# Routed attention followed by a channel mix: moving the weight loads, two cluster products and the token shift within the loop

## Chip, cores and metric

One core of a Trainium2 chip. The metric is the device time of one execution in microseconds (us). Ratios are the mean time of one kernel's fast runs over that of the other's fast runs of the same rounds, so not quite the ratio of the medians quoted. A run counts as slow when it lies over 1.5% above the fastest of its kernel.

## The reference, cut to what matters

```python
# attention over 4 batches x 8 heads, 768 positions, head_dim 64, 16 clusters a head
q_assign = argmax(normed(q) @ normed(centroids).T); k_assign = the same of k
mask   = q_assign[:, None] == k_assign[None, :]
x      = softmax(where(mask, q @ k.T / 8, -1e9)) @ v      # -> (4, 768, 512)
# channel mix
x_prev = x shifted by one position
xk, xr = mu_k * x + (1 - mu_k) * x_prev,  mu_r * x + (1 - mu_r) * x_prev
k      = maximum(xk @ w_k, 0)
out    = sigmoid(xr @ w_r) * (k * k @ w_v)
```

The mask is made by arithmetic: each position's cluster, as 16 one-hot rows, is appended to q and k ("aug"), so the score matmul adds a bonus where clusters agree.

## The kernel before

Heads go in 16 pairs. The loop has 192 steps of one score product (two matmuls, lines 286 and 287), one exponential and six value matmuls; a pair n takes steps 12n to 12n+11. Everything else is hung on step numbers: `at(t, f)` puts f at the end of step t, `forced[t]` in its middle. That makes the order of the code for each engine and each issuing queue. Slices of the channel mix fill PE from step 58 on.

```python
at(6, load_mu)                                   # two 2 KB vectors, SP's queue
for i in range(4):
    at(9 + i, load_wk, i)                        # key weights: cast to bf16, issued by GpSimd
    at((19, 20, 28, 29)[i], load_wv, 2 * i)      # value weights
for i in range(2):
    at(37 + i, load_wr, 2 * i)                   # receptance weights
...
for n in range(NPAIR):
    s = n * W                                    # W = 12
    ...
    # a: steps (from s) of four DVE transposes of pair n+2's q and k, and of its cluster products
    if n == NP:       a = (8, 9, 10, 11, 14)     # NP = 4
    elif n == NP + 1: a = (3, 4, 5, 6, 10)
    elif n == NP + 2: a = (1, 2, 3, 4, 8)
    else:             a = (-1, 0, 1, 2, 5)
    for g in range(4): at(s + a[g], trans, n + 2, g)
    forced[s + a[4]] = lambda n=n: aff_mm(n + 2) # on PE, reads all four transposes
    d = a[4] - 4
    at(s + 5 + d, aff_max, n + 2)                # DVE: maximum, comparison
    at(s + 6 + d, aff_back, n + 2, [nc.sync])    # DVE transpose, then four one-hot transfers on SP
    at(s + 8, load_v, n + 2, nc.sync)
    ...
    e = s + W + NCH                              # = s + 18
    at(e, xt_dma, n); x = e + 4                  # pairs 4 to 14 (the change leaves 7 and 11 at e + 4)
    at(x, sh); at(x + 1, sh2)                    # token shift on DVE: six instructions
```

(Cut: the first pairs' own paths, where PE transposes.)

The softmax here doesn't subtract the row's maximum and nothing guards it: scores larger than these inputs give would overflow.

## Time and profile before

| | before |
|---|---|
| time, median of 4 runs | 255.16 us (253.51 to 257.03) |
| span of the profiled run | 254.8 us |
| PE, ACT, DVE busy | 95%, 74%, 69% |
| mean granted TensorE clock | 0.993 |

The shares are averages over stages with different limits; what counts is which wait ends last in a stage. I therefore read the profile in stretches of twelve steps, bounded by the starts of the score matmuls of line 286. The prediction shows these stretches.

### The profile page before, as it was taken

What the parts mean: (1) busy time and instruction counts of PE and PEld (TensorE: products, weight loads), DVE (VectorE), ACT (ScalarE), POOL (GpSimd) and SP (SyncE); (2) the same over time, 40 slices, a digit from 0 to 9 for tenths busy, and PEclk for the clock granted to TensorE, in tenths of its full rate; (3) what the DMA queues carried; (4) which work ended last, traced back from release to release, by engine and by line L of the source; (5) the groups of instructions that cost most, each with busy time, mean ns of one, the idle gap of its engine ahead of it and who ended that gap; (6) DMA issues with size and microseconds to landing.
All of it is one profiled execution on the core that took longest, in us unless ns stands there. A gap on an engine that the chain in (4) does not pass through costs nothing.

```text
span 254.8 us, 6199 instructions
## 1 busy us (share of the span) xinstructions
PE 243.2 (95%) x2356; PEld 148.2 (58%) x2387; DVE 176.6 (69%) x375; ACT 189.7 (74%) x271; POOL 94.0 (37%) x186
## 2 busy tenths in 40 slices
PE   7999979999999999999999999999999999999994
PEld 3866747766665554555666655555666555555441
DVE  3476765998999979676979877767776356554222
ACT  4298967989998867787889986878999887146210
POOL 2877867581644263543261607070701000000000
PEclk9999997999999999999999999999999999999999
DMA  6782999798938385869674949496222112120122
GB/s 177 210 238 32 199 279 244 126 140 147 185 46 162 57 159 102 162 158 195 157 115 108 129 104 204 119 193 104 74 47 65 44 71 73 47 79 0 56 110 85
DMA packets 102318, 31.88 MB, mean 125 GB/s; under 512 B 74704, under 2 KB 98704, under 8 KB 102288
## 3 DMA queue, kind: packets, MB, share of 16 engines
q1 hardware_dynamic: 98352, 28.03, 52.6%
q0 software_dynamic: 2208, 2.62, 6.4%
q10 hardware_dynamic: 1728, 0.82, 1.2%
q8 instruction: 19, 0.31, 0.5%
q14 instruction: 11, 0.09, 0.1%
HBM read 24.15 MB, written 6.29 MB: 119 GB/s over the span
## 4 chain that ended last, share of the span: by engine, by line
PE 74%; DMA 8%; ACT 7%; DVE 4%; issue 3%; POOL 2%; SPq 1%; DVEq 0%; ACTq 0%
PE psv L405 16%; PE st L286 13%; PE out L299 11%; PE psr L394 8%; PE psk L382 8%; PE st L287 6%; ACT pt L289 6%; DMA qk_nat<-in_q_dram 4%; PE affps L194 4%; PE psk L373 4%; DMA qk_rows<-in_q_dram 2%; PE trps L161 2%; DVE qkT L145 1%; DMA cn_sb<-in_centroids_dram 1%; POOL aug L175 1%
## 5 line engine op out<-in xcount | busy, mean ns | idle before, releaser
L289 ACT ACTIVATE pt<-st 128x768 bf16<-128x768 f32 x192 | 148.4, 811 | 26.0 <-PE st L287 25.5
L175 POOL TENSOR_SCALAR aug<-qkT 64x384 bf16<-64x384 f32 x128 | 68.3, 533 | 85.5 <-DVE qkT L145 58.5
L299 PEld LDWEIGHTS <-pt 128*128 128x128 bf16 x1152 | 60.4, 97 | 27.2 <-ACT pt L289 1.7
L286 PE MATMUL st<-aug 80*128 80x512 bf16 x192 | 73.7, 384 | 1.6 <-ACT pt L289 0.5
L299 PE MATMUL out<-vt,pt 128*128 128x65 bf16 x1152 | 66.6, 193 | 1.1 <-ACT pt L289 0.8
L287 PE MATMUL st<-aug 80*128 80x256 bf16 x192 | 52.2, 272 | 0.0
L405 PE MATMUL psv<-w_v_sb,k 128*128 128x512 bf16 x181 | 46.3, 378 | 0.8 <-ACT tanh L397 0.2
L387 ACT ACTIVATE kr<-psk 128x512 bf16<-128x512 f32 x48 | 28.8, 600 | 8.6 <-PE psk L382 4.7
L409 DVE SCALAR_TENSOR_TENSOR out_sb<-tanh,psv 128x512 f32<-128x512 bf16 x24 | 16.3, 680 | 27.1 <-PE psv L405 26.6
L382 PE MATMUL psk<-xk,w_k_sb 128*128 128x512 bf16 x113 | 30.6, 378 | 0.7
L388 DVE TENSOR_TENSOR k<-kr 128x512 bf16<-128x512 bf16 x48 | 21.9, 459 | 13.4 <-ACT kr L387 13.3
L286 PEld LDWEIGHTS <-aug 80*128 80x128 bf16 x192 | 18.8, 98 | 16.3 <-issue 8.4
L397 ACT ACTIVATE tanh<-psr 128x512 bf16<-128x512 f32 x24 | 14.3, 597 | 18.1 <-PE psr L394 14.6
L405 PEld LDWEIGHTS <-k 128*128 128x128 bf16 x192 | 16.8, 97 | 16.8 <-issue 2.0
L287 PEld LDWEIGHTS <-aug 80*128 80x128 bf16 x192 | 19.1, 99 | 9.9 <-issue 1.7
L394 PE MATMUL psr<-w_r_sb,xr 128*128 128x512 bf16 x91 | 23.7, 379 | 0.2
L182 POOL CAST vt<-v_nat 128x384 bf16<-128x384 f32 x32 | 16.3, 539 | 14.2 <-DMA v_nat<-in_v_dram 13.3
L145 DVE STREAM_TRANSPOSE qkT<-qk_nat 128x384 f32<-128x384 f32 x40 | 20.6, 550 | 0.0
L312 DVE TENSOR_TENSOR xn<-out,rs 128x384 bf16<-128x384 f32 x32 | 17.8, 557 | 1.1
L373 PE MATMUL psk<-xk,w_k_sb 128*128 128x256 bf16 x128 | 16.6, 272 | 0.4 <-DVE out_sb L409 0.4
L382 PEld LDWEIGHTS <-w_k_sb 128*128 128x128 bf16 x128 | 11.2, 97 | 9.3
L194 PE MATMUL affps<-qkT,cblk 128*32 128x384 f32 (+1 forms) x144 | 15.6, 445 | 0.0
(64 smaller groups left out, 196.4 us busy)
## 6 DMA issues: line engine op xcount, KB each, us to landing
v_nat<-in_v_dram SPq DMA_DIRECT2D x16, 384.0 KB, 4.0
out_dram<-out_sb SPq DMA_DIRECT2D x24, 256.0 KB, 2.6
qk_nat<-in_q_dram SPq DMA_DIRECT2D x40, 96.0 KB, 4.0
qk_nat<-in_k_dram SPq DMA_DIRECT2D x40, 96.0 KB, 3.5
qk_rows<-in_q_dram SPq DMA_DIRECT2D x5, 384.0 KB, 5.6
qk_rows<-in_k_dram SPq DMA_DIRECT2D x4, 384.0 KB, 6.2
aug<-oht SPq DMA_DIRECT2D x60, 24.0 KB, 1.9
w_k_sb<-in_moe_w_k_dram POOLq DMA_DIRECT2D x4, 256.0 KB, 5.8
```

Source lines behind the costliest of these rows:

```text
L145: nc.vector.transpose(qkT[n][:, g, :], nat[n][:, g // 2, (g % 2) * GW:(g % 2 + 1) * GW])
L175: nc.gpsimd.tensor_scalar(augv(n, g)[0:64, par, :], in0=qkT[n][64 * par:64 * par + 64, g, :], scalar1=qk_scale, scalar2=1.0, op0=ALU.mult, ...
L194: nc.tensor.matmul(ps[32 * g:32 * g + 32, u], cblk[:, 2 * j + g % 2, :, :], qkT[n][:, g, u], start=True, stop=True, tile_position=(0, 32 * g))
L286: nc.tensor.matmul(st[:, 0:512], kc, a[rows, 0:512], start=True, stop=True)
L287: nc.tensor.matmul(st[:, 512:S], kc, a[rows, 512:S], start=True, stop=True)
L289: nc.scalar.activation(pt, st, AF.Exp, bias=-BIG, scale=BIG)
L299: nc.tensor.matmul(o[:, (qc + NCH // 2) % NCH, :], pts[bh * NCH + c][:, qc * 128:(qc + 1) * 128], vts[n % NR][:, tt, 2 * (c % 3) + c // 3, ...
L373: nc.tensor.matmul(ps[:, a * 256:(a + 1) * 256], w_k_sb[:, j, (i + a) * 128:(i + a + 1) * 128], self.xk[:, j, 512:768], start=(j == 0), st ...
L382: nc.tensor.matmul(ps, w_k_sb[:, j, ii * 128:(ii + 1) * 128], self.xk[:, j, 0:512], start=(j == 0), stop=(j == NJ - 1))
L387: nc.scalar.activation(kr, src, AF.Relu)
L394: nc.tensor.matmul(ps, self.xr[:, j, sl], w_r_sb[:, j, :], start=(j == 0), stop=(j == NJ - 1))
L405: nc.tensor.matmul(self.psvt, self.k2[:, i, sl], w_v_sb[:, i, :], start=(i == 0), stop=(i == NI - 1))
```

## The change

Its intent: load the key weights while the DMA engines are nearly idle (52 GB/s in 19 to 26 us of the profile before, 191 in 26 to 32), so that pair 4's rows come in time; give pair 8's and 9's transposes time before PE needs them; move DVE work (the token shift) away from them.

```diff
-    krp = ctx.enter_context(tc.tile_pool(name="krp", bufs=3))
+    krp = ctx.enter_context(tc.tile_pool(name="krp", bufs=5))
...
-            at(9 + i, load_wk, i)
-            at((19, 20, 28, 29)[i], load_wv, 2 * i)
+            at(7 + i // 2, load_wk, i)
+            at((27, 28, 39, 40)[i], load_wv, 2 * i)
...
-            at(37 + i, load_wr, 2 * i)
+            at(50 + i, load_wr, 2 * i)
...
-                        a = (1, 2, 3, 4, 8)
+                        a = (1, 2, 3, 4, 9)
+                    elif n == NP + 3:
+                        a = (0, 1, 2, 3, 8)
...
-                x = e + 4
+                x = e + (4 if n % NP == NP - 1 else 7)
```

## The prediction

> **What bounds the kernel now.** I counted the loop's steps by the score matmuls of line 286: one starts each step, 192 in all, then a tail without them. Their start times in the timeline give the borders of every twelve steps, and the view of engine busy time by windows gives what filled each stretch. Columns: length of the stretch, busy time of PE, weight loads, DVE, ACT and POOL, granted TensorE clock, DMA share, GB/s. Here are steps 12, 24, 36, 48, 60, 72, 84, 96 and 108 with the twelve steps that follow each:
>
> ```profile
> 22.46:32.51 10.05, 10.05 (x138) 6.89 (x139) 7.00 (x15) 8.97 (x13) 9.04 (x17) 1.00 0.84 152
> 32.51:45.60 13.09, 11.18 (x135) 7.98 (x131) 8.97 (x16) 8.95 (x13) 9.55 (x18) 0.87 1.14 260
> 45.60:55.43 9.83, 9.56 (x135) 6.85 (x131) 9.15 (x18) 9.18 (x13) 6.71 (x12) 1.00 0.76 124
> 55.43:64.34 8.91, 8.15 (x103) 5.55 (x102) 8.03 (x20) 8.83 (x13) 2.12 (x4) 1.00 0.95 149
> 64.34:78.77 14.43, 14.27 (x146) 8.64 (x148) 14.26 (x32) 12.88 (x19) 9.07 (x17) 1.00 0.67 109
> 78.77:94.37 15.60, 15.29 (x142) 9.01 (x144) 13.15 (x29) 12.54 (x19) 6.49 (x12) 1.00 0.67 119
> 94.37:108.31 13.94, 13.66 (x132) 7.74 (x132) 11.50 (x24) 9.89 (x14) 5.34 (x10) 1.00 0.71 145
> 108.31:122.22 13.91, 13.80 (x140) 7.84 (x139) 10.20 (x23) 11.26 (x16) 5.00 (x10) 1.00 0.78 164
> 122.22:135.29 13.07, 12.91 (x138) 8.24 (x140) 10.98 (x25) 11.69 (x18) 5.47 (x10) 1.00 0.70 133
> ```
>
> The reader is to see three regimes. Up to step 60 a step takes about 0.76 us, and ACT's exponential (811 ns by the page, a little less when two run together) sets it. From step 60 a step with a slice of the second operator takes 1.37 us and one without takes 0.51; PE is busy throughout, and this goes on to the end. Between them lie the odd stretches: 32.51 to 45.60 costs 3 us more than either neighbour, and 78.77 to 94.37 costs more than the same work later. PE being "busy" there hides waits inside a group of matmuls.
>
> Next, the waits in 30 to 46 us, the timeline at step 26, and the windows cut around it:
>
> ```profile
> PE trps L161 <- DMA qk_rows<-in_q_dram: 1.6, 1, 1.6
> ...
> 36.27 0.41 PE L161 MATMUL trps<-ident,qk_rows 128*128 128x128 f32 x2 [1.64 <-DMA qk_rows<-in_q_dram]
> ...
> 34.30:37.83 3.53, 1.89 (x29) 1.51 (x27) 2.21 (x4) 1.78 (x3) 1.97 (x3) 1.00 1.18 272
> 37.83:41.24 3.41, 3.41 (x28) 2.59 (x24) 1.70 (x4) 2.29 (x4) 2.26 (x4) 0.50 1.15 271
> 41.24:45.60 4.36, 4.35 (x66) 2.85 (x63) 3.44 (x7) 3.35 (x6) 3.70 (x7) 1.00 1.12 220
> ```
>
> PE stands still for 1.64 us until pair 4's query rows land, and the next 3.41 us run at half the clock. One late transfer is paid for twice.
>
> Why it is late shows in the DMA view of 26 to 32 us, and in the timeline where PE meets pair 8:
>
> ```profile
> q0 software_dynamic: 506, 0.94, 93.4%
> q1 hardware_dynamic: 350, 0.19, 11.0%
> ...
> 88.26 2.05 PE L194 MATMUL affps<-qkT,cblk 128*32 128x384 f32 x8
> 88.68 0.14 PEld L194 LDWEIGHTS affps<-qkT,cblk 128*32 128x32 f32 x2 [0.28 <-DVE qkT L145]
> 89.48 0.14 PEld L194 LDWEIGHTS affps<-qkT,cblk 128*32 128x32 f32 x2 [0.66 <-DVE qkT L145]
> ```
>
> Just before and while the rows are issued (30.52), the software queue, which carries the key weights, holds 93% of the DMA engines' time; the rows move only from about 32.5. In 19 to 26 us the same view shows 52 GB/s: the engines were almost idle there. The last two lines are the second place: the cluster products of pair 8 wait for DVE's transposes.
>
> [...] their issues cost POOL time: 562 ns median for the key weights here.
>
> **The change, part by part.** *Key weights at steps 7 and 8 rather than 9 to 12.* Same four issues, another place. In POOL's program order two now come before the value casts of pair 1 and two just after. From the timeline POOL ends the casts ahead of them at 21.5, so the issues fall at about 21.6 to 22.9 and 23.9 to 25.1, against 23.8 to 25.0 and 27.9 to 29.0. The software queue moved 0.94 MB in 6 us; 1 MB needs about 6 us, plus 1.5 us for the 384 KB of values in between. Landed by about 31 (estimate) instead of 34.7. *The value weights* leave steps 19, 20, 28, 29 for 27, 28, 39, 40, so none is in the way before step 27; *the receptance weights* go to step 50. *Pair 4's rows behind pair 2's one-hot transfers:* in the program order of SP they stand there already, with and without the change; this part costs and gains nothing. Issued at 30 to 30.5, the rows should need what a less loaded transfer needed: 3.5 us (issued 9.8, landed 13.3) to 4.1 us (14.6 to 18.6). That is 33.8 to 34.5; PE comes for them at 36.27 - 1.64 = 34.6. So the stall goes, or shrinks to a few tenths, and with it the half clock. The worth: 13.09 minus the neighbours' mean (10.05 + 9.83) / 2 = 9.94 makes 3.15; I take 2.8 for the thin margin. POOL's own delay of 1.3 us at step 7 falls on casts needed at steps 18 and 24: beside other work.
>
> *Cluster products of pair 8 one step later (81 for 80).* Steps 72 to 84 hold eight slices and one set of products, like steps 96 to 108: 15.60 - 13.91 = 1.7 us of excess. By step starts, 1.3 of it is at step 80 and 0.3 at step 78, where ACT waits for DVE to free a buffer (0.7 us, ACT kr L387 <- DVE k L388). One step is worth 1.37 us if it carries a slice and DVE has the same work ahead of the last transpose, so nearly all of the wait is covered. *The kr ring of 5* takes away that ACT wait. I count 1.4 for the two.
>
> *Pair 9: transposes one step later, products three steps later (92 for 89).* Steps 84 to 96: seven slices and products, like steps 108 to 120 at 13.07; 13.94 - 13.07 = 0.87. I count 0.7. *The token shift three steps later* adds no work. It moves about 3 us of DVE work behind the one-hot chain and spares DVE's wait for the transposed tile (2.1 us in 78 to 95), so it helps the same two places and is not counted again.
>
> Sum: 2.8 + 1.4 + 0.7 = 4.9 us. All of it lies on the path, since every step after follows PE or ACT in order, and the steps from 96 on are unchanged.
>
> **The rivals.** *First: the rows stay late.* The key weights start only 2.2 us earlier, and the one-hots and values share the engines with them. If the weights still flow at 31, the rows land near 35.5, one microsecond of stall remains and perhaps the half clock: gain 2.5 to 3 in all, time about 253. For it: a margin of at most 0.8 us. Against: the idle engines before 26 us, and no value weights at 31.35. *Second: the displaced weights hurt what they now meet.* The later value and receptance weights now share 45 to 58 us with pair 6's rows in small pieces, which feed DVE, the busiest engine there (14.26 of 14.43). If DVE's transposes come 1 to 2 us late, time is about 252.5. Against: pair 6 landed before 60 and DVE took it up at 63.84, behind its own queue. *Third: DVE is the bound from 46 to 92 us*, so the later products only meet the same transposes: steps 72 to 84 would gain 0.4 rather than 1.4, time about 252. *Fourth: all of it works fully* (3.15 + 1.7 + 0.87, and a little at step 70): about 250.
>
> **Range and chances.** The profiled execution took 256.6 us by its own time, so 4.9 less is 251.7. The three timed runs average 255.4, and part of their spread (253.51 to 257.03) may be whether the half clock struck, worth up to 1.7; taking half of 1.2 as already absent leaves 255.4 - 4.3 = 251.1. I say 251.2, nearer the second, as timed runs are what counts. Two per cent under 255.74 is 250.6, half a microsecond below my value, so faster by over 2% is somewhat less likely than not. Slower needs a new stall of 10 us with the gains, which nothing suggests. Range 248.8 to 253.9.
>
> **What would show it right or wrong.** Right: no PE wait for qk_rows between 30 and 40 us, no half-clock window there, steps 24 to 36 in about 10 us, the eight products of pairs 8 and 9 back to back in 0.85 to 1.0 us, steps 72 to 84 in about 14.2 and 84 to 96 in about 13.2, and everything from step 96 as long as before. Wrong: software-queue traffic still at 31 us with PE waiting on the rows; a new wait at step 36, 48 or 60 on a one-hot or on pair 6; or DVE idle time replaced by DVE lateness at step 81. If timed runs before never saw the half clock, my gain is too large by 0.6.

## The result, and the profile after

264.18 us median of 4 runs (262.35 to 264.83), ratio 1.034 (95% interval 1.025 to 1.043): slower. The profiled run's span is 263.1 us, 8.2 more than before.

The windows view of the kernel after, by its own steps 12, 24, 48, 60, 72, 84, 96 and 120 (columns as in the prediction):

```profile
21.84:34.45 12.61, 10.28 (x139) 6.98 (x140) 9.25 (x20) 9.16 (x12) 8.12 (x17) 1.00 0.96 179
34.45:45.72 11.27, 10.99 (x131) 7.89 (x132) 6.85 (x12) 8.54 (x12) 8.58 (x16) 0.85 0.93 207
...
55.55:67.34 11.79, 8.15 (x102) 5.50 (x102) 10.15 (x24) 9.48 (x13) 3.68 (x8) 0.99 1.14 173
67.34:82.81 15.47, 15.15 (x145) 8.99 (x149) 12.14 (x26) 12.34 (x18) 9.39 (x18) 0.90 0.70 110
82.81:96.75 13.94, 13.78 (x143) 8.63 (x144) 12.93 (x28) 12.43 (x19) 6.67 (x12) 1.00 0.72 134
96.75:110.04 13.29, 13.10 (x131) 7.51 (x132) 10.36 (x21) 9.77 (x14) 5.45 (x10) 1.00 0.80 165
110.04:126.00 15.96, 14.63 (x140) 7.98 (x139) 12.89 (x26) 11.26 (x16) 5.15 (x10) 1.00 0.60 132
...
139.07:155.36 16.29, 14.87 (x144) 8.88 (x144) 11.37 (x24) 12.97 (x20) 5.39 (x10) 1.00 0.62 93
```

Lengths against before, stretch by stretch: steps 12 to 24 +2.56, 24 to 36 -1.82, 48 to 60 +2.88, 60 to 72 +1.04, 72 to 84 -1.66, 84 to 96 -0.65, 96 to 108 +2.05, 120 to 132 +2.36, 132 to 144 +1.28, 144 to 156 +0.35; start, first steps and tail together -0.2; the rest is equal. The sum is the 8.2 of the spans. Two things are to be seen: gains came where they were forecast (72 to 96, and in part 24 to 36), and losses came in three other places: at step 24, at step 60, and at step 101 with three later steps like it.

**Two waits for one-hots.** The timeline of the kernel after, at the first score matmuls of steps 24 and 60 (in brackets the idle time before, and what ended it):

```profile
34.45 0.38 PE L286 MATMUL st<-aug 80*128 80x512 bf16 x1 [2.01 <-DMA aug<-oht]
...
67.34 0.61 PE L286 MATMUL st<-aug 80*128 80x512 bf16 x1 [2.92 <-DMA aug<-oht]
```

Its chain of waits around both (start, length, what):

```profile
26.86 0.51 SPq L219
27.43 6.93 DMA aug<-oht
...
60.31 6.98 DMA aug<-oht
```

The two transfers of 24 KB took 6.93 and 6.98 us. Pair 4's rows, which were late before, are in time now; pair 2's one-hots, issued just ahead of them on SP's queue, have become the late ones, and so have pair 5's. With each wait came a half-clock window again: the granted clock was 0.50 from 36.30 to 39.71 us and from 67.02 to 70.43 (0.85 over steps 24 to 36, 0.90 over 60 to 72). The DMA view tells what stood before pair 2's one-hots. Before, in 22.2 to 29.5 us (count, KB each, median us from issue to landing):

```profile
v_nat<-in_v_dram SPq DMA_DIRECT2D x1, 384.0 KB, 3.6
aug<-oht SPq DMA_DIRECT2D x5, 24.0 KB, 3.8
mu_k_sb<-in_moe_mu_k_dram SPq DMA_DIRECT2D x1, 2.0 KB, 2.3
mu_r_sb<-in_moe_mu_r_dram SPq DMA_DIRECT2D x1, 2.0 KB, 2.3
```

After, in 21.5 to 29.2 us:

```profile
v_nat<-in_v_dram SPq DMA_DIRECT2D x1, 384.0 KB, 10.9
aug<-oht SPq DMA_DIRECT2D x5, 24.0 KB, 6.6
mu_k_sb<-in_moe_mu_k_dram SPq DMA_DIRECT2D x1, 2.0 KB, 5.7
mu_r_sb<-in_moe_mu_r_dram SPq DMA_DIRECT2D x1, 2.0 KB, 5.9
```

mu went out before the key weights in the kernel before, and its four-byte packets were through in 2.3 us. Now the key weights flow at that moment: their issues start at 21.0 us and mu's at 21.7, where before mu's started at 22.4 and theirs at 23.8.

**DVE before pair 10's products.** The timeline before, around step 101:

```profile
107.75 0.36 DVE L349 TENSOR_TENSOR diff<-xt 128x384 bf16<-128x384 bf16 x1 [0.36 <-DMA xt<-xn]
...
110.96 1.49 DVE L145 STREAM_TRANSPOSE qkT<-qk_nat 128x384 f32<-128x384 f32 x3
...
114.05 0.85 PE L194 MATMUL affps<-qkT,cblk 128*32 128x384 f32 x8
```

And after:

```profile
111.77 1.03 DVE L145 STREAM_TRANSPOSE qkT<-qk_nat 128x384 f32<-128x384 f32 x2
112.72 0.49 DVE L349 TENSOR_TENSOR diff<-xt 128x384 bf16<-128x384 bf16 x1
...
115.07 0.56 DVE L145 STREAM_TRANSPOSE qkT<-qk_nat 128x384 f32<-128x384 f32 x1
...
117.23 0.56 DVE L145 STREAM_TRANSPOSE qkT<-qk_nat 128x384 f32<-128x384 f32 x1
117.85 0.14 PEld L194 LDWEIGHTS affps<-qkT,cblk 128*32 128x32 f32 x2 [1.92 <-DVE qkT L145]
```

The token shift of pair 6 stood ahead of all four transposes of pair 10; now it stands between the second and the fourth, and PE waits for the fourth. The same order costs 2.4 us at step 125, 1.3 at 137 and 0.35 at 149.

### The profile page after: what moved, and what is told of

Read it like the earlier page. It is cut to its first block, busy times and chain, and to the rows that moved or that the text cites. A ratio compares the mean times of both kernels' runs of the same rounds, so it can differ in the third digit from the quotient of the medians.

```text
span 263.1 us, 6208 instructions
## 1 busy us (share of the span) xinstructions
PE 244.4 (93%) x2356; PEld 148.4 (56%) x2387; DVE 181.1 (69%) x375; ACT 189.7 (72%) x271; POOL 94.4 (36%) x186
## 4 chain that ended last, share of the span: by engine, by line
PE 67%; DVE 13%; DMA 11%; issue 4%; SPq 2%; ACT 1%; DVEq 0%; ACTq 0%
PE psv L405 13%; PE st L286 11%; PE psk L382 9%; PE out L299 8%; DMA aug<-oht 6%; PE psr L394 5%; PE st L287 5%; PE psk L373 5%; PE affps L194 4%; DMA qk_nat<-in_q_dram 3%; DVE qkT L145 2%; SPq L219 2%; PE wps L446 2%; DVE out_sb L409 2%; DVE oht L217 1%
## 5 line engine op out<-in xcount | busy, mean ns | idle before, releaser
L409 DVE SCALAR_TENSOR_TENSOR out_sb<-tanh,psv 128x512 f32<-128x512 bf16 x24 | 16.3, 679 | 28.5 <-PE psv L405 27.2
L388 DVE TENSOR_TENSOR k<-kr 128x512 bf16<-128x512 bf16 x48 | 21.2, 444 | 18.5 <-ACT kr L387 18.4
L382 PE MATMUL psk<-xk,w_k_sb 128*128 128x512 bf16 x113 | 31.2, 385 | 0.9 <-issue 0.2
L286 PEld LDWEIGHTS <-aug 80*128 80x128 bf16 x192 | 18.9, 98 | 21.7 <-issue 11.3
L397 ACT ACTIVATE tanh<-psr 128x512 bf16<-128x512 f32 x24 | 14.4, 599 | 18.3 <-PE psr L394 17.4
L405 PEld LDWEIGHTS <-k 128*128 128x128 bf16 x192 | 16.8, 97 | 17.2 <-issue 2.4
L182 POOL CAST vt<-v_nat 128x384 bf16<-128x384 f32 x32 | 16.3, 539 | 20.7 <-DMA v_nat<-in_v_dram 19.9
L145 DVE STREAM_TRANSPOSE qkT<-qk_nat 128x384 f32<-128x384 f32 x40 | 21.4, 556 | 0.0
L194 PE MATMUL affps<-qkT,cblk 128*32 128x384 f32 (+1 forms) x144 | 16.5, 445 | 3.0 <-DVE qkT L145 3.0
```

The lines of the kernel that those rows point to most:

```text
L145: nc.vector.transpose(qkT[n][:, g, :], nat[n][:, g // 2, (g % 2) * GW:(g % 2 + 1) * GW])
L194: nc.tensor.matmul(ps[32 * g:32 * g + 32, u], cblk[:, 2 * j + g % 2, :, :], qkT[n][:, g, u], start=True, stop=True, tile_position=(0, 32 * g))
L286: nc.tensor.matmul(st[:, 0:512], kc, a[rows, 0:512], start=True, stop=True)
L382: nc.tensor.matmul(ps, w_k_sb[:, j, ii * 128:(ii + 1) * 128], self.xk[:, j, 0:512], start=(j == 0), stop=(j == NJ - 1))
L405: nc.tensor.matmul(self.psvt, self.k2[:, i, sl], w_v_sb[:, i, :], start=(i == 0), stop=(i == NI - 1))
```

## The experiments

Lengths in us of the stretches that differ, from each run's own profile (one profiled execution each), and the timed ratio:

| run | 0-12 | 12-24 | 24-36 | 48-60 | 60-72 | 72-84 | 84-96 | 96-108 | 120-156 | ratio (95% interval) |
|---|---|---|---|---|---|---|---|---|---|---|
| before | 10.4 | 10.1 | 13.1 | 8.9 | 14.4 | 15.6 | 13.9 | 13.9 | 40.9 | 1 |
| after | 10.7 | 12.6 | 11.3 | 11.8 | 15.5 | 13.9 | 13.3 | 16.0 | 44.9 | 1.034 (1.025-1.043) |
| e1_weights_only | 10.4 | 11.9 | 9.7 | 11.2 | 16.8 | 15.2 | 14.4 | 13.9 | 40.9 | 1.005 (0.998-1.013) |
| e2_shift_only | 10.4 | 10.1 | 13.2 | 8.9 | 14.9 | 15.1 | 14.4 | 15.1 | 44.9 | 1.013 (1.004-1.021) |
| e3_products_ring | 10.4 | 10.1 | 12.9 | 9.1 | 14.7 | 14.4 | 13.8 | 18.5 | 40.9 | 1.007 (0.998-1.016) |
| e4_products_ring_shift45 | 10.4 | 11.5 | 14.8 | 8.9 | 14.7 | 13.9 | 13.3 | 14.9 | 41.2 | 0.993 (0.981-1.004) |
| h1_weights_free_queue | 12.0 | 10.1 | 10.0 | 11.3 | 14.7 | 15.5 | 14.3 | 13.9 | 41.4 | 1.014 (0.999-1.029) |
| h2_weights_wr_back | 10.4 | 12.5 | 9.7 | 9.9 | 15.6 | 15.2 | 14.1 | 13.9 | 40.9 | 1.008 (0.999-1.016) |
| h3_pair8_ring_shift4 | 10.4 | 11.1 | 15.2 | 9.3 | 14.5 | 13.9 | 14.8 | 13.9 | 40.9 | 1.006 (0.994-1.019) |
| h4_pair8_wk_first | 14.5 | 12.0 | 9.7 | 8.9 | 14.7 | 13.9 | 14.8 | 13.9 | 40.9 | 1.013 (1.004-1.021) |
| k1_weights_v_on_act | 10.7 | 16.8 | 11.5 | 12.0 | 16.3 | 15.1 | 14.0 | 13.9 | 40.9 | 1.031 (1.023-1.040) |
| k2_wk_mu_v_on_act | 10.5 | 10.1 | 10.3 | 9.0 | 14.9 | 15.5 | 14.0 | 13.9 | 40.9 | 0.994 (0.986-1.001) |
| k3_repaired | 10.3 | 10.1 | 10.1 | 8.9 | 14.9 | 13.9 | 13.3 | 14.9 | 40.9 | 0.990 (0.985-0.996) |
| k4_repaired_pair10 | 10.3 | 10.1 | 9.9 | 9.3 | 14.8 | 13.9 | 13.3 | 13.9 | 40.9 | 0.977 (0.970-0.984) |

A warning on the ratios: the kernel before itself ran between 253.1 and 261.1 us in the later rounds. Its runs at a granted clock of 0.997 or more took 253.1 to 255.9, those at 0.986 or 0.987 took 257.5 to 260.2, and the wait at steps 24 to 27 is as changeable: e4 and h3, which load the weights as before, took 26.3 and 26.2 us for steps 12 to 36 where the profile of before had 23.1 (for e4 that puts the profiled run, 258.97 us, among its slow ones; only its later stretches are used). Differences under 1% are therefore read from the stretches, not from the ratio. All runs were correct.

### One part at a time

**e1_weights_only**: the kernel before with the three weight lines of the diff.

> The kernel before with the weight moves alone (key weights at steps 7 and 8, value weights at 27, 28, 39, 40, receptance weights at 50). Theory Q (queue order: weights on the software queue starve the small packets on SP's queue, and pair 2's and pair 5's one-hot transfers wait behind them): a wait of about 2.5 us at step 24 and about 3.5 us at step 60, each followed by a half-clock window, the stall at step 26 gone; about 5 us slower than before. Rival D (the whole loss comes from the token shift on DVE): the same time as before or 2 to 3 us faster, as the prediction had it.

Measured: waits at steps 21 and 23 (1.1 and 0.8 us over the length before), 59 and 60; the wait at step 26 gone; half clock only after step 60 (the run's granted clock was 0.987). The weights alone take 3.0 us more than before from the first to the last step. Of the first two, step 21 is DVE waiting 0.7 us for mu, with PE behind it, and step 23 the one-hots (0.7 us). So a loss comes from the weights, of 3 rather than 5 us. Rival D falls by these waits in the trace; the timed ratio alone, 1.005 (0.998 to 1.013), would not exclude it.

**e2_shift_only**: `x = e + (4 if n % NP == NP - 1 else 7)` and nothing else.

> The kernel before with the token shift three steps later and nothing else. Theory S (the shift now lies on DVE between the transposes of the pair two later and the products that need them): waits of PE for DVE at steps 101, 125, 137 and 149 that sum to about 6 us, and some more at step 89, where the products of pair 9 have not been moved here; 6 to 8 us slower. Rival Q alone (all loss from the weights): the same time as before, or up to 1 us faster.

Measured: steps 96 to 108 +1.2, 120 to 156 +4.0, in sum 5.2 us, at exactly the steps named, and 0.4 more in 84 to 96. Timed, 1.3% slower, about 3 us: less than the 6 to 8 expected. In the traces the shift is the largest single loss.

**e3_products_ring**: pair 8's and 9's tuples and the ring of 5.

> The kernel before with the products of pairs 8 and 9 later and the ring of five, shift and weights untouched. If the prediction's steps for these parts are right, steps 72 to 84 shrink by about 1.5 us and 84 to 96 by about 0.7 us: 2 us faster than before. If DVE is the bound there and the products only meet the same transposes, under 0.7 us faster.

Steps 72 to 84 shrink by 1.2; 84 to 96 hardly; and, not expected by either theory, steps 96 to 108 grow by 4.6. A half-clock window (113.9 to 117.3 us; the run's granted clock was 0.987) is part of that. Its waits in 100 to 125 us:

```profile
DVE diff L349 <- DMA xt<-xn: 2.6, 1, 2.6
```

The later products of pair 9 put their DVE chain (maximum, comparison, transpose: about 2.1 us by the durations in the timelines) and a wait for pair 6's transposed tile in front of pair 10's transposes. So the products of pair 9 moved on their own cost more at step 101 than they bring at 89.

**e4_products_ring_shift45**: the same with

```diff
-                x = e + 4
+                x = e + (7 if n in (NP, NP + 1) else 4)
```

> As the run with products and ring, with the shift three steps later for pairs 4 and 5 alone, whose products' deadlines were moved too. Theory S: no waits at steps 101, 125, 137, 149, and up to 0.5 us faster than without the shift. If a later shift hurts wherever it stands: slower than without it by 1 us or more.

Steps 120 to 144 are as before; 144 to 156 lose 0.3 (DVE waited 0.6 us for the transfer that frees an output buffer, as in h1, without any late shift); 72 to 96 as short as in the kernel after; 96 to 108 at 14.9. Steps 96 to 108 are about 3.6 us shorter than in e3, far more than the 0.5 us expected, so most of e3's loss needed the shift of pairs 4 and 5 at its old place as well as pair 9's later products. A later shift is good for pairs 4 and 5 and bad for the later ones, as theory S says; against its expectation, a wait of 1 us is left at step 101.

### What held the one-hots

**h1_weights_free_queue**: e1 with `at(4, load_mu)` and pair 2's `load_v` on `nc.scalar` at step 8.

> The weight moves alone, with the two mu vectors loaded at step 4 (while the engines are idle) and pair 2's values loaded through ACT's queue, so that nothing large stands before pair 2's one-hot transfers on SP's queue; the key weights flow at the same time as in the weights-only run. Theory Q (the one-hots were late because they stood behind mu and values on the same queue): the one-hots land 4 to 5 us after issue, as in the kernel before, no wait at steps 21 and 24; steps 12 to 24 take 10.0 to 10.6 us instead of 11.9; the wait at step 60 stays. Rival R (the engines are simply full with weights, whatever the queue): the one-hots land as late as before, near 33 us, and steps 12 to 24 still take 11.5 us or more.

Steps 12 to 36 take 20.0 us, no half clock (granted clock 1.000); theory Q's part held. But steps 0 to 12 grew by 1.7: ACT issued the values at 18.2 us, before pair 1's one-hots, for which PE then waited 1.9 us at step 12. The transfer that was taken off the queue met other one-hots instead. The wait at 59 stayed, as expected.

**h2_weights_wr_back**: e1 with `at(37 + i, load_wr, 2 * i)`.

> The weight moves with the receptance weights back at steps 37 and 38. If the receptance weights at step 50 make pair 5's one-hots late: the waits at steps 59 and 60 fall from 3.5 us in sum to under 1 us and there is no half-clock window after 60 us. If the value weights at 39 and 40 do: they stay. The wait at step 24 stays in both.

Steps 48 to 60 fell from 11.2 to 9.9 and 60 to 72 from 16.8 to 15.6, but not to 8.9 and 14.4, and a half-clock window stayed (the run's granted clock was 0.993): between the two answers expected. Of e1's 4.6 us of loss in 48 to 72, 2.4 went. So the receptance weights at 50 make about half of it. The rest is put down to the value weights at 39 and 40: no run moves these alone, but h4 and k2, with both moved back, keep at most 0.5 us of it.

**h4_pair8_wk_first**: h3 (below) with `at(3 + i // 2, load_wk, i)`, `at(4, load_mu)` and value weights at 27 to 30.

> As the run before it, and the key weights at steps 3 and 4, with mu before them and the value weights at 27 to 30: the weights then flow in the idle stretch before pair 2's values and one-hots are issued. If the prediction's idea was right and only its place on the queue wrong: no wait for pair 4's rows at step 26, no half clock there, at most 0.5 us more at step 12 because pair 1's one-hots meet the weights; 2.5 to 3.5 us faster than the run before it. If not: pair 1's one-hots land 2 us or more late and step 12 pays what step 26 gains.

The bad case came: pair 1's one-hots had nothing large before them on their own queue (mu stood there, but had landed by about 20 us, when the one-hots began to go out), and still took 5.8 us (its DMA view in 17.5 to 21.5 us), where 1.9 was usual:

```profile
aug<-oht SPq DMA_DIRECT2D x4, 24.0 KB, 5.8
```

Steps 0 to 12 grew by 4.1 us. Rival R is thus partly right: beside the running stream of weights these small transfers took 5.8 us even on a free queue. The rest of the idea held: no wait at 24 or 26 (12 to 24 took 12.0 us, which I put down to a half clock after the wait at step 12; the run's granted clock was 0.984).

**k1_weights_v_on_act**: e1 with only pair 2's values moved, to ACT at step 12.

> The weight moves alone, with pair 2's values taken off SP's queue: issued by ACT at step 12, after pair 1's one-hots are through (in the run with the free queue they were issued at 18.2 us and met those one-hots instead). mu stays where it was. Queue order (Q): pair 2's one-hots land within 4 us of issue, steps 0 to 12 take 10.4 us, steps 12 to 24 at most 10.6, 24 to 36 under 10, with no half clock there; the wait at step 60 stays. If the place of the values was not what held the one-hots: step 24 still waits over 1.5 us.

My expectation failed, in an informative way: steps 12 to 24 took 16.8 us. mu, still on SP's queue at step 6, now shared the engines with two streams: in 21 to 29 us the software queue with the key weights held 61.5% of the engines' time, ACT's queue with the values 17.3%, SP's 10.3%. Its DMA view in 21 to 29 us, and its waits in 24 to 40 us:

```profile
mu_k_sb<-in_moe_mu_k_dram SPq DMA_DIRECT2D x1, 2.0 KB, 6.1
mu_r_sb<-in_moe_mu_r_dram SPq DMA_DIRECT2D x1, 2.0 KB, 10.3
```

```profile
DVE mu_r_sb L508 <- DMA mu_r_sb<-in_moe_mu_r_dram: 4.7, 1, 4.7
PE xtps L327 <- DVE qkT L169: 4.7, 1, 4.7
```

A vector of 2 KB took 10.3 us, DVE stood before it for 4.7 us, and PE behind DVE. The four-byte packets of mu were at the head of the queue, and the values, one-hots and rows behind them; taking away the values alone did not help.

### Settling and repairing

**h3_pair8_ring_shift4**: the kernel before with pair 8's tuple, the ring of 5, and the shift later for pair 4 alone.

> The kernel before with pair 8's products one step later, the ring of five, and the shift three steps later for pair 4 alone; pair 9 and all later pairs untouched. Theory: moving pair 9's products put their DVE chain in front of pair 10's transposes, and that was the loss at step 101; so here steps 96 to 108 take 13.9 us as before and steps 72 to 84 take 13.9 to 14.4: 1 to 1.7 us faster than before in the trace. Rival: pair 10's wait comes from elsewhere and steps 96 to 108 stay above 14.8.

Steps 96 to 108 are back at 13.9 and 72 to 84 at 13.9: the wait at step 101 did come from pair 9's products. But 84 to 96 grew to 14.8, since pair 9's products, left at step 89, now wait for transposes behind pair 8's later chain. The waits hand on from pair to pair; the trace is no faster than before, as it also fell on a bad wait at step 26.

**k2_wk_mu_v_on_act**: key weights at 7 and 8, mu on ACT's queue at step 6, pair 2's values on ACT's queue at step 12, value weights at 27 to 30, receptance weights at 37 and 38.

> A repair of the weight moves: key weights at 7 and 8, mu and pair 2's values on ACT's queue, value weights at 27 to 30, receptance weights at 37 and 38 as before. If both waits are told rightly (step 24: SP's queue held; step 60: weights issued after 50 us): no wait at 24, 26, 59 and 60, no half clock, steps 12 to 36 together 19.7 to 20.6 us instead of 23.1, steps 48 to 60 8.9 us; about 2.5 to 3 us faster than the kernel before. If weights in flight hurt whatever their queue: one of these waits stays, and the time is that of before.

Steps 12 to 36 take 20.3 us against 23.1, 48 to 60 are as before, and every run was at a clock of 0.999 or more (252.75 to 254.03 us). Both waits are gone. This confirms that order and company on the queues made them, not the earlier key weights as such. It is a repair in several parts at once: mu went out on ACT's queue at 16.8 us and was through in 2.4 us, before the first key weights at 20.6, so its new time may count as much as its new queue. Timed, k2 is 0.6% faster, inside the noise (0.986 to 1.001), not the 2.5 to 3 us expected.

**k3_repaired**: k2's weights with e4's products, ring and shift.

> The same repair of the weights together with pair 8's and pair 9's products later, the ring of five and the shift later for pairs 4 and 5 alone. If the parts add: steps 12 to 36 about 20 us, steps 72 to 108 about 42.1 us, nothing lost after step 108; 3.5 to 4.5 us faster than the kernel before, the fastest of all. If they don't: at best the better of the two parts alone.

252.47 us median (251.92 to 253.23), ratio 0.990. The parts add in the trace (72 to 108: 42.1 us); timed, the gain is 1%, about 2.5 us, less than the 3.5 to 4.5 us expected.

**k4_repaired_pair10**: k3 with

```diff
+                    elif n == NP + 4:
+                        a = (-1, 0, 1, 2, 6)
```

> The repaired version with pair 10's products one step later too (step 102 for 101). Theory: the wait of 1 us left at step 101 is pair 10's last transposes, which stand on DVE behind pair 9's one-hot chain since pair 9's products come three steps later; one step of 1.37 us covers it: steps 96 to 108 take 13.9 us instead of 14.87, nothing new later, about 0.9 us faster than the repaired version. Rival: DVE is the bound there and the wait moves to step 102 or to pair 11 at step 113: the same time.

251.22 us median of 6 runs (250.46 to 252.59) beside 259.33 for all 11 runs of before in the same rounds (255.85 to 260.13); ratio of the fast runs 0.977. Windows of k3 for steps 96 to 108:

```profile
102.64:117.51 14.87, 14.74 (x142) 7.97 (x139) 11.95 (x26) 11.26 (x16) 5.37 (x10) 1.00 0.62 131
```

And of k4 for steps 12 to 36 and 72 to 108:

```profile
21.04:31.10 10.06, 10.06 (x139) 6.90 (x139) 7.38 (x15) 9.10 (x13) 9.08 (x18) 1.00 0.85 171
31.10:41.04 9.94, 9.54 (x135) 6.82 (x132) 8.37 (x16) 8.66 (x13) 7.06 (x13) 1.00 1.11 251
...
74.93:88.87 13.94, 13.94 (x146) 8.64 (x144) 13.03 (x28) 12.44 (x19) 7.21 (x12) 1.00 0.72 133
88.87:102.16 13.29, 13.21 (x133) 7.51 (x132) 10.37 (x21) 9.77 (x14) 5.46 (x10) 1.00 0.82 175
102.16:116.07 13.91, 13.91 (x142) 7.72 (x139) 11.17 (x25) 11.26 (x16) 5.03 (x10) 1.00 0.68 140
```

This version beats the kernel before clear of noise (0.970 to 0.984), and with it the kernel after. The wait of a microsecond at step 101 is gone and did not move on.

## Why the prediction was wrong, step by step

The sum was 4.9 us gained, with nothing lost elsewhere. Three of its steps failed: that the token shift "adds no work" and leaves "the steps from 96 on" unchanged (6.0 us lost), that the displaced weights cost nothing (3.9 us lost in 48 to 72), and that the order on SP's queue "costs and gains nothing" (2.6 us lost in 12 to 24). Together that is 12.5 us, more than the "new stall of 10 us" that nothing seemed to suggest.

**The wait at step 26.** "So the stall goes" was right: pair 4's rows landed in time, and no step waited for them. The failing step is the account of SP's queue before it: that pair 4's rows stand behind pair 2's one-hots already, so that "this part costs and gains nothing". I asked only when the rows would land. I did not ask what else SP's queue held while the weights flowed earlier: mu, values, one-hots, in that order, each needed sooner than the rows. In the kernel after, mu, the values and the one-hots, all on SP's queue, landed in the order of their issue: issued at 21.7, 22.98 and 26.86 us, landed near 27.4, 33.9 and 34.4. The half clock, which was to go with the stall, came back with the new wait of 2.01 us. Steps 24 to 36 gained 1.82 of the 2.8 counted, and 12 to 24 lost 2.56. My first rival had the right kind of failure, a thin margin in a shared queue, for the wrong transfer.

**The displaced weights.** The second rival named the right stretch and asked after pair 6's rows and a loss of 1 to 2 us. The transfer that came late was pair 5's one-hots, the loss 2.88 + 1.04 us with a half-clock window, and h2 puts about half of e1's like loss on the receptance weights. In the list of what would show me wrong I had "a new wait at step 36, 48 or 60 on a one-hot"; I gave it no weight in the sum. I also misread the stretch: "14.26 of 14.43" is DVE in steps 60 to 72; in 48 to 60, where the weights flow, DVE was busy for 8.03 of 8.91 us and ACT for 8.83.

**The token shift.** "Adds no work ... not counted again" and "the steps from 96 on are unchanged" are the largest error. The diff changes the shift for pairs 6, 8, 9 and 10 too. The pairs four later (10, 12, 13, 14) have their transposes at -1 to 2, and the shift, three steps later, falls among them. e2 shows 5.2 us for it alone; in the kernel after the same steps lose 6.0, the rest being pair 9's chain at step 101 (e4, k4). The prediction works its place out for pairs 8 and 9 alone. The timeline shows that no transpose passed the shift: DVE ran its six instructions from 112.72 us and pair 10's last two transposes, which stand among and after them in the code, at 115.07 and 117.23, and PE waited 1.92 us for the last.

**Pairs 8 and 9.** 1.4 and 0.7 us were predicted, 1.66 and 0.65 measured. For pair 8's wait the mechanism was right: step 80 shrank by 1.2 us (its excess was 1.2, not the 1.3 of the prediction). The rest is in part luck. The 0.46 at steps 78 and 79 also came in e2, without the ring of 5, so what the ring is worth was not shown; it was never run alone. Of the 0.65, 0.34 came at step 86, in e2 and e4 too, but not in e3 and h3, so from pair 5's later shift; pair 9's later products themselves brought 0.3, since steps 91 and 92 took back most of step 89's gain. What was missed is that a product moved later moves its one-hot chain on DVE later as well, and that this chain then stands before the next pair's transposes (e3: steps 96 to 108 grew by 4.6 us; h3: 84 to 96 by 0.9).

**The sum.** About my 4.9 us (2.8 + 1.4 + 0.7) were there to be had, by k4's other order: in its trace steps 12 to 36 gain 3.1, 72 to 84 gain 1.7, 84 to 96 gain 0.65, less 0.7 lost in 48 to 72, 4.7 in all. The prediction was the value of the intent, and the change as written paid three new waits for it.

**What stays open.** Whether h4's one-hots (median of four 5.8 us beside the key weights, 1.9 in the kernel before) were late by packet size or by something behind the engines: no run separates them. Nor does a run move mu alone, or use the ring of 5 alone. What decides whether a wait brings a half clock was not shown either: a wait of 1.64 us in the kernel before, with PE busy for 1.89 of 3.53 us, was followed by one, and a wait of 2.01 us in the kernel after; h1 had a wait of 1.9 us at step 12, and steps 48 to 60 took 2.4 us more than before, at a granted clock of 1.000 over its profiled run, so the length of the wait alone does not decide.

## What to carry to other kernels

When a transfer is moved into an idle stretch of the DMA engines, list everything that is queued there and behind it, with the step that needs each; the most urgent small transfer, not the one that was late before, decided here (pair 2's one-hots, a wait of 2.01 us). When a line with a step number serves many iterations, work out where it falls among the other numbered work in each of them, above all on an engine that works in the order of the code, as DVE did here from 112.72 to 117.23 us. And put tiny loads (here two vectors of 2 KB in four-byte packets, through in 2.3 us in the kernel before, in 5.7 and 5.9 beside the key weights, in 6.1 and 10.3 in k1) where nothing urgent stands behind them on the queue.
